# Thirteen units' second-order terms by seven block products, with softmax parts on GpSimd: an attention and MLP kernel on one core

## The chip, the cores and the metric

The program runs on one core of one Trainium2 chip. The metric is device time of one execution in microseconds (us). A core has TensorE (PE; PEld is its weight load), VectorE (DVE), ScalarE (ACT), GpSimd (POOL) and SyncE (SP, which here only starts transfers).

## The reference

Eight batches, eight heads, 576 tokens, 64 numbers per head; the inputs q and k are scaled by 200.

```
a = exp(phi - max(phi, axis=2)); a = a / (sum(a, axis=2) + 1e-09)        # 32 memory slots per head
k_m = einsum('bhsm,bhsd->bhmd', a, k); v_m = einsum('bhsm,bhsd->bhmd', a, v)
attn = softmax(q @ k_m.T / sqrt(64))                                      # over the 32 slots
x = (attn @ v_m), as 4608 tokens x 512
h = x @ w_in (512 x 2048);  g = h - tanh(h);  out = g @ w_out (2048 x 512)
```

## The kernel before

**Numbers in two halves.** Every float32 operand of the large products is kept as a float16 high part and a float16 low part (the rest), and a product is three products: high x high, high x low and low x high; low x low is left out. S_W, S_G and the like are powers of two that keep the parts in float16's range. The weights come as float64 bit patterns, and are turned into float32 and split in the start.

**Tiles.** Tokens go in 18 units of 256 (u), the 2048 inner columns in four blocks of 512 (fb). One *slot* is one pair (u, fb):
- *First product*, `mm1` (line 434): the weights are folded into the attention first (`att_p`, line 403, makes P = v_m w_in for a batch and fb), so h is P times the softmax: four column chunks k, six matmuls each over 256 tokens, into the accumulator tile h. There are two of these (pool `ps_h`, two buffers).
- *g = h - tanh(h)* by a polynomial: ScalarE squares h into u (line 450), VectorE makes h3 from h and u (458), ScalarE squares u once more (459), VectorE multiplies (464), ScalarE writes the float16 high part (466), VectorE the low part (471).
- *Second product*, `mm2` (line 483), for the slot two before: for each of two halves of 128 tokens and four chunks k, three matmuls of 512 columns (g high by w_out high and low, g low by w_out high) into the accumulators o0 and o1, which collect over the four fb of a unit. After the fourth ScalarE scales them to SBUF (line 516) and SyncE stores them.

**Order.** Up to the middle of unit 4 the order of all engines is written out as a list of words (START) and kept by `in_order`. T, E, L, K turn weights into float16 parts, i and o load them; H, a, b, c, M are first product, polynomial and second product. In this start units 0 to 3 keep partial sums in DRAM, which GpSimd's queue stores. From slot 18 on (unit 4, fb 2) a loop runs over the slots, and each batch's attention is hung in at slots before the batch's first: FX, FA, Q, KV load phi (twice), q, keys and values; X and Y take a maximum over phi, subtract it and apply exp; V pools keys and values (line 147, 80 matmuls); N, U, UV normalise and turn; S makes scores (187); A and B are the softmax (205 to 222); BH and BL its high and low parts (393, 399); P and PL make P (411 to 423). There the scheduler may order the instructions. The loop also reads all weights a second time (chk) and tests on ScalarE (309, 310) that none is out of the split's range; `squares_in`, `norms_in` and their like test norms. If a test fails, a wide path, not run here, does all in float32.

## Time and profile before

| | us |
|---|---|
| median of three runs | 696.89 |
| lowest, highest | 694.16, 697.13 |
| the profiled execution | 696.4 |
| its span, first to last instruction | 694.6 |
| TensorE busy | 664.5 |
| VectorE busy | 477.4 |
| ScalarE busy | 398.3 |
| GpSimd busy | 10.8 |

The span is divided into busy time per engine, into 40 slices, and into the chain of work that ended last. A group's row names line, engine, operation, output and inputs with their sizes, and behind the bar busy time, mean ns of one and the idle time in front. Matmuls overlap in the records: one of 512 columns is shown as 379 ns although the next starts 0.216 us after it, so the distance of starts is what counts.

### The profile page before, as it was taken

Reading aid. Unit: us, or ns where it says so; the run is one execution under the profiler, and the core shown is the slowest. Engines: PE = TensorE matmul, PEld = TensorE weight load, DVE = VectorE, ACT = ScalarE, POOL = GpSimd, SP = SyncE. Lnnn points to the kernel's source line nnn. Section 1 sums busy time; section 2 is a strip of 40 time slices with the busy share of each in tenths; the row PEclk is TensorE's granted clock in tenths of the full one; section 3 lists DMA queues with packets and bytes.
Section 4 is the critical chain, followed back from the end, with each engine's and each line's share of the span. In section 5 each row is a group of like instructions: output and inputs, shape, how many; then the busy total and the mean of one; then the engine's idle time right before and its main releaser. Section 6 shows DMA issues by size and latency. Waiting matters only on the chain.

```text
span 694.6 us, 13671 instructions
## 1 busy us (share of the span) xinstructions
PE 664.5 (96%) x5992; PEld 392.1 (56%) x5992; DVE 477.4 (69%) x571; ACT 398.3 (57%) x526; POOL 10.8 (2%) x26
## 2 busy tenths in 40 slices
PE   2688999999999999999999999999999999999996
PEld 2345574664656556666555655665566555666552
DVE  6699999998976596446596559556955695444541
ACT  3447666664545865665865595556645664544341
POOL 0000000001000000000000000000000000000000
PEclk9799999999999999999999999999999999999999
DMA  9955534682413940002940195009200300000001
GB/s 322 361 200 202 194 130 156 205 278 77 148 62 108 341 130 6 27 16 89 344 131 2 59 361 157 2 32 331 96 1 31 123 32 1 32 1 32 1 30 36
DMA packets 34003, 84.87 MB, mean 122 GB/s; under 512 B 3472, under 2 KB 8208, under 8 KB 33936
## 3 DMA queue, kind: packets, MB, share of 16 engines
q1 hardware_dynamic: 32512, 79.59, 33.3%
q0 software_dynamic: 1280, 4.20, 1.6%
q8 instruction: 49, 0.80, 0.5%
q14 instruction: 18, 0.15, 0.1%
q10 hardware_dynamic: 144, 0.13, 0.1%
HBM read 72.37 MB, written 11.53 MB: 121 GB/s over the span
## 4 chain that ended last, share of the span: by engine, by line
PE 78%; DVE 17%; DMA 3%; issue 1%; ACT 1%; SPq 0%; DVEq 0%
PE o L498 47%; PE h L444 22%; PE pkv L147 3%; PE pp L411 3%; DVE wt L264 2%; DVE wt L268 2%; DVE h L458 2%; DVE h L464 2%; DVE wt L260 1%; DMA kv<-in_kva_dram 1%; PE psc L187 1%; DVE g L471 1%; DVE ph L423 1%; DVE wout_lo L295 1%; DMA chk<-in_w_out_dram 1%
## 5 line engine op out<-in xcount | busy, mean ns | idle before, releaser
L498 PE MATMUL o<-wout_hi,g 128*128 128x512 f16 x1152 | 354.4, 379 | 0.8 <-ACT g L466 0.8
L498 PEld LDWEIGHTS <-g 128*128 128x128 f16 x1728 | 164.2, 98 | 206.9 <-issue 16.7
L498 PE MATMUL o<-wout_lo,g 128*128 128x512 f16 x576 | 218.4, 379 | 0.0
L444 PE MATMUL h<-ah,ph 128*128 128x256 f16 (+3 forms) x1536 | 201.2, 246 | 0.4 <-DVE h L458 0.4
L444 PEld LDWEIGHTS <-ph 128*128 128x128 f16 x2304 | 178.6, 98 | 28.9 <-issue 2.5
L444 PE MATMUL h<-al,ph 128*128 128x256 f16 (+3 forms) x768 | 170.1, 246 | 0.0
L458 DVE SCALAR_TENSOR_TENSOR h<-h,u 128x1024 f32<-128x1024 f32 x72 | 87.5, 1218 | 67.6 <-ACT u L450 67.6
L450 ACT ACTIVATE u<-h 128x1024 f32<-128x1024 f32 x72 | 73.2, 1018 | 91.5 <-PE h L444 91.5
L471 DVE TENSOR_TENSOR g<-h,g 128x1024 f16<-128x1024 f32 x70 | 85.3, 1221 | 49.8 <-ACT g L466 49.8
L466 ACT ACTIVATE g<-h 128x1024 f16<-128x1024 f32 x72 | 76.0, 1056 | 72.9 <-DVE h L464 72.9
L459 ACT ACTIVATE u<-u,beta 128x1024 f32<-128x1024 f32 x72 | 82.6, 1147 | 51.3 <-DVE h L458 50.6
L464 DVE SCALAR_TENSOR_TENSOR h<-u,h 128x1024 f32<-128x1024 f32 x72 | 87.9, 1221 | 25.8 <-ACT u L459 24.5
L423 DVE SCALAR_TENSOR_TENSOR ph<-pp,ph 128x1024 f16<-128x1024 f32 x32 | 38.9, 1216 | 2.4 <-ACT ph L418 2.4
L418 ACT ACTIVATE ph<-pp 128x1024 f16<-128x1024 f32 x32 | 32.5, 1016 | 1.9 <-PE pp L411 1.9
L516 ACT ACTIVATE ot<-o 128x512 f32<-128x512 f32 x35 | 20.5, 588 | 14.3 <-PE o L498 14.2
L147 PE MATMUL pkv<-kv,e 128*32 128x129 f32 (+1 forms) x640 | 25.6, 294 | 2.6 <-DMA kv<-in_kva_dram 2.2
L196 DVE STREAM_TRANSPOSE sc<-psc 128x288 f32<-128x288 f32 x32 | 13.5, 459 | 19.6 <-PE psc L187 19.6
L309 ACT ACTIVATE fy<-chk 128x512 f32<-128x512 f32 x32 | 21.4, 667 | 5.2 <-DMA chk<-in_w_in_dram 2.8
L310 ACT ACTIVATE fy<-fy,one 128x512 f32<-128x512 f32 x32 | 23.0, 719 | 0.7
L147 PEld LDWEIGHTS pkv<-kv,e 128*32 128x32 f32 (+1 forms) x640 | 17.1, 114 | 10.8 <-issue 5.9
L264 DVE SCALAR_TENSOR_TENSOR wt<-raw,wt 128x512 uint32<-128x512 uint32 x32 | 20.7, 688 | 0.0
L268 DVE SCALAR_TENSOR_TENSOR wt<-raw,wt 128x512 uint32<-128x512 uint32 x32 | 20.6, 687 | 0.0
(96 smaller groups left out, 372.3 us busy)
## 6 DMA issues: line engine op xcount, KB each, us to landing
kv<-in_kva_dram SPq DMA_DIRECT2D x32, 516.0 KB, 7.7
q<-in_qt_dram SPq DMA_DIRECT2D x16, 576.0 KB, 7.0
raw<-in_w_in_dram SPq DMA_DIRECT2D x16, 512.0 KB, 6.6
raw<-in_w_out_dram SPq DMA_DIRECT2D x16, 512.0 KB, 5.1
chk<-in_w_in_dram SPq DMA_DIRECT2D x16, 512.0 KB, 5.0
chk<-in_w_out_dram SPq DMA_DIRECT2D x16, 512.0 KB, 5.3
out_dram<-ot SPq DMA_DIRECT2D x27, 256.0 KB, 2.0
pt<-in_phx_dram SPq DMA_DIRECT2D x8, 576.0 KB, 4.4
```

The lines of the kernel that those rows point to most:

```text
L147: nc.tensor.matmul(pa[32 * h : 32 * h + 32, r, 0:129], e[0:K, c, 32 * hh : 32 * hh + 32], d["kv"][h][0:K, r, c, :], start=(c == 0), stop=( ...
L264: nc.vector.scalar_tensor_tensor(t, r[:, :, 0], 29, t, op0=ALU.logical_shift_right, op1=ALU.bitwise_or)
L268: nc.vector.scalar_tensor_tensor(t, r[:, :, 1], 0xC0000000, t, op0=ALU.bitwise_and, op1=ALU.bitwise_or)
L423: nc.vector.scalar_tensor_tensor(pl, pa, S_P / (S_V * S_W), ph, op0=ALU.mult, op1=ALU.subtract)
L444: nc.tensor.matmul(hp[:, k, tu : tu + w], px[:, g, cs], d[ax][:, g, ta : ta + w], start=(n == 0), stop=(n == 5),)
L450: nc.scalar.activation(uu, hp, AF.Square, scale=1.0 / (S_A * S_P))
L458: nc.vector.scalar_tensor_tensor(h3, hp, C2 * S_G / (S_A * S_P), uu, op0=ALU.mult, op1=ALU.mult)
L459: nc.scalar.activation(uu, uu, AF.Square, bias=c["beta"])
L464: nc.vector.scalar_tensor_tensor(h3, uu, CC, h3, op0=ALU.add, op1=ALU.mult)
L466: nc.scalar.activation(gg[:, 0], h3, AF.Copy)
L471: nc.vector.tensor_tensor(gg[:, 1], h3, gg[:, 0], op=ALU.subtract)
L498: nc.tensor.matmul(o, gx[:, k, P * tt : P * tt + P], wx[:, 4 * fb + k, :], start=(first and k == 0 and wx is wout_hi and gx is gh), stop=( ...
```

## The change

**Second product.** From unit 5 on `mm2_blocks` takes the place of `mm2`. High x high stays: 2 x 4 matmuls of 512 columns. The two second-order terms together are the product of a 2 x 2 block matrix by another: g in blocks by token half (th) and pair of chunks (kh), w_out by pair of chunks and column half (nh), both with a high and a low layer. Eight block products become seven, in Strassen's scheme, each of four matmuls of 256 columns: high of one side by low of the other and the reverse, for two chunks. Sums of w_out's blocks (`b_form`, words G in the start) are made once, on GpSimd, in float16, in tiles bt that take the place of the key and value buffers; sums of g's blocks (`a_forms`) in each slot, by four VectorE instructions on 512 float16 numbers per partition. Four of the products go into a tile x, which takes one of the two buffers of `ps_h`; first products keep one, hs. At a unit's end (`evict`) x is added to both accumulators' results: two copies on ScalarE, six steps on VectorE.

**GpSimd.** It makes g's low part, the softmax subtraction and division, the softmax's low part, phi's subtraction for batches 4 to 7, and the squares of the weight test.

**Plan.** The whole program keeps the written order. Attention of a batch is spread over 14 slots by a table, in halves: keys and values are loaded for the first half r = 0, pooled, and then for r = 1 into the same buffers; words before ";" stand behind the first product, those between ";" and "|" behind the second product's matmuls, the rest at the slot's end. Batch 3's phi maximum and first loads stand at the end of START. S_W and S_G are smaller powers of two.

```diff
-S_W = 2.0 ** 14
+S_W = 2.0 ** 13
-S_G = 2.0 ** 25
+S_G = 2.0 ** 23
...
-M31 L15 PL03 b02 T13 o13:gg H22 V2 N2 b12 H03 L13 c02 P13 c12 PL13 M02 a03 o12:pp4 U2 a22 T14 b03 H13 L14 c03
+PL03 b02 T13 o13:gg H22 V2 N2 b12 H03 L13 G00 c02 P13 c12 PL13 G01 M02 a03 o12:pp4 U2 G02 a22 T14 b03 H13 G03
...
+    def load_kv_half(self, b, d, r):
...
+        for g in range(2):
+            t = self.big.tile([P, 2, 5, 129], F32, tag="q", name=f"kv{b}{g}{r}")
+            for i in range(2):
+                nc.sync.dma_start(t[:, i, 0:4, :], ins["kva"][b, 2 * g + i, :, r])
+                nc.sync.dma_start(t[0:64, i, 4, :], ins["kvt"][b, 2 * g + i, :, r])
...
+    def expo_pool(self, b, d):
...
+        nc.scalar.activation(m[:, 0], d["px"][:, 0, 0:256], AF.Copy)
+        nc.gpsimd.tensor_tensor(e[:, 0:4, :], e[:, 0:4, :], m.to_broadcast((P, 4, 256)), op=ALU.subtract)
...
+    def soft_max(self, b, d, t):
...
+        nc.vector.tensor_reduce(m, s3, axis=AX.X, op=ALU.max)
+        nc.gpsimd.tensor_tensor(s3, s3, m.unsqueeze(2).to_broadcast((P, NB, 32)), op=ALU.subtract)
...
     def window(k):
...
-        nc.scalar.activation(y, hf, AF.Square)
+        nc.gpsimd.tensor_tensor(y, hf, hf, op=ALU.mult)
...
+    def g3_pool(u, fb):
+        h3, gg = gs[u, fb]
+        nc.gpsimd.tensor_tensor(gg[:, 1], h3, gg[:, 0], op=ALU.subtract)
...
+    def a_block(gg, th, kh):
+
+        return gg[:, :, 2 * kh : 2 * kh + 2, P * th : P * th + P]
+    def a_forms(u, fb):
+
+        gg = gs[u, fb][1]
+        a11, a21, a12, a22 = (a_block(gg, th, kh) for kh in range(2) for th in range(2))
+        f = big.tile([P, 2, 4, 2, P], F16, tag="uu", name=f"f{u}{fb}")
+        s4, s3, s1, s2 = (f[:, :, i] for i in range(4))
+        for o, x, y, op in ((s3, a21, a11, ALU.subtract), (s1, a21, a22, ALU.add), (s2, s3, a22, ALU.add), (s4, a12, s2, ALU.subtract)):
+            nc.vector.tensor_tensor(o, x, y, op=op)
...
+    def b_form(fb, i):
+
+        if i == 0:
+            bts[fb] = big.tile([P, 4, 2, 2, 256], F16, tag=f"kv{fb}", name=f"bt{fb}", bufs=1)
+        for n, w in enumerate((wout_hi, wout_lo)):
...
+            nc.gpsimd.tensor_tensor(t[:, i, n], x, y, op=ALU.subtract)
...
+    def mm2_blocks(u, fb, first, last):
...
+        def main(th):
+            for k in range(4):
+                nc.tensor.matmul(
+                    o[th], gg[:, 0, k, P * th : P * th + P], wout_hi[:, 4 * fb + k, :], start=(first and k == 0), stop=False
+                )
+
+        def prod(dst, a, b, new=False, end=False):
+            for kk in range(2):
+                for n in range(2):
+                    nc.tensor.matmul(
+                        dst, a(1 - n, kk), b(n, kk), start=(new and kk == 0 and n == 0), stop=(end and kk == 1 and n == 1)
+                    )
...
+        m1 = (x[:, 0, lo], ab(0, 0), bb(0, 0), first)
+        m2 = (o[0][:, lo], ab(0, 1), bb(1, 0))
+        m3 = (o[0][:, hi], af(0), bb(1, 1))
+        m4 = (o[1][:, lo], ab(1, 1), bf(3))
+        m5 = (x[:, 0, hi], af(2), bf(0))
+        m6 = (x[:, 1, lo], af(3), bf(1), first)
+        m7 = (x[:, 1, hi], af(1), bf(2))
+        if not last:
+            main(0)
+            main(1)
+            for m in (m2, m4, m1, m5, m6, m7, m3):
+                prod(*m)
+            return
...
+        for m, end in ((m1, False), (m5, True), (m6, False), (m7, True)):
+            prod(*m, end=end)
+        nc.scalar.activation(ra[:, 1], x[:, 0, lo], AF.Copy, scale=sc)
+        nc.scalar.activation(rb[:, 2], x[:, 0, hi], AF.Copy, scale=sc)
+        for th, ms in ((0, (m2, m3)), (1, (m4,))):
+            main(th)
+            for m in ms:
+                prod(*m, end=m is ms[-1])
...
+    def evict():
...
+        nc.vector.scalar_tensor_tensor(ra[:, 0], x[:, 1, lo], sc, ra[:, 1], op0=ALU.mult, op1=ALU.add)
+        nc.vector.scalar_tensor_tensor(rb[:, 0], x[:, 1, hi], sc, ra[:, 0], op0=ALU.mult, op1=ALU.add)
+        nc.vector.tensor_tensor(ra[:, 2], ra[:, 0], rb[:, 2], op=ALU.add)
+        nc.vector.tensor_tensor(rb[:, 1], rb[:, 0], rb[:, 2], op=ALU.add)
...
+            nc.vector.scalar_tensor_tensor(r, o[th], sc, r, op0=ALU.mult, op1=ALU.add)
+            nc.sync.dma_start(out[t0 + P * th : t0 + P * th + P, :], r)
...
+        (-11, "FQ{0} FA{0}"), (-10, "; X{0} KR{0}0"), (-9, "| XP{0} YM{0}"), (-8, "; YE{0} | V{0}0 KR{0}1 N{0}0"), (-7, "| V{0}1 N{0}1 QT{0}0"),
...
+        mm1(u, fb)
+        g1(u, fb)
+        do(0)
+        g1_square(u, fb)
+        if forms:
+            a_forms(*forms.pop())
+        g2(u, fb)
+        queue.append((u, fb))
+        v, vb = queue.pop(0)
+        (mm2 if v < 5 else mm2_blocks)(v, vb, vb == (2 if v in parts else 0), vb == NFB - 1)
+        while squared:
+            window_sum(*squared.pop(0))
+        do(1)
+        g2_high(u, fb)
+        g3_pool(u, fb)
+        while due:
+            step(due.pop(0), True)
+        evict()
+        if u > 4:
+            forms.append((u, fb))
+        do(2)
```

How it moves instructions, at three places. First TensorE in the second product of unit 16, fb 0 (g160 is that slot's g, high and low part; o1600 and o1601 are the accumulators). Before, 24 such pairs of a weight load and a matmul of 512 columns:

```order
L498 LDWEIGHTS g160_7111
L498 MATMUL o1600_7275<-wout_hi_96,g160_7111 128x512
...
L498 MATMUL o1600_7275<-wout_lo_97,g160_7111 128x512
...
L498 MATMUL o1601_7276<-wout_hi_96,g160_7111 128x512
...
L498 MATMUL o1601_7276<-wout_lo_97,g160_7111 128x512
```

Now eight pairs of the leading term and 28 of the products (bt0 holds sums of w_out's blocks, f160 sums of g's):

```order
L668 LDWEIGHTS g160_8065
L668 MATMUL o1600_8207<-wout_hi_96,g160_8065 128x512
...
L668 MATMUL o1601_8208<-wout_hi_96,g160_8065 128x512
...
L675 MATMUL o1600_8207<-wout_lo_97,g160_8065 128x256
...
L675 MATMUL o1601_8208<-bt0_1644,g160_8065 128x256
...
L675 MATMUL x_2678<-wout_hi_96,g160_8065 128x256
...
L675 LDWEIGHTS f160_8105
L675 MATMUL x_2678<-bt0_1644,f160_8105 128x256
...
L675 MATMUL o1600_8207<-wout_hi_96,f160_8105 128x256
```

The leading term stands ahead of all that needs g's low part, and the products that need the sums of the slot's g come last.

Second VectorE in the slot of unit 16, fb 1, in which unit 15 ends. Before, with the weight test's last steps between:

```order
L458 SCALAR_TENSOR_TENSOR h3161_7185<-h161_7158,u161_7183 128x1024
L346 TENSOR_REDUCE stat_65<-wn_6931 128x4
...
L464 SCALAR_TENSOR_TENSOR h3161_7185<-u161_7183,h3161_7185 128x1024
L471 TENSOR_TENSOR g161_7189<-h3161_7185,g161_7189 128x1024
L458 SCALAR_TENSOR_TENSOR h3162_7268<-h162_7241,u162_7266 128x1024
```

Now:

```order
L547 SCALAR_TENSOR_TENSOR h3161_8102<-hs_2679,u161_8100 128x1024
L583 TENSOR_TENSOR f160_8105<-g160_8065 128x2x256 x2
L583 TENSOR_TENSOR f160_8105<-f160_8105,g160_8065 128x2x256
L583 TENSOR_TENSOR f160_8105<-g160_8065,f160_8105 128x2x256
L556 SCALAR_TENSOR_TENSOR h3161_8102<-u161_8100,h3161_8102 128x1024
L724 SCALAR_TENSOR_TENSOR r150_8111<-x_2678,r150_8111 128x256
L725 SCALAR_TENSOR_TENSOR r151_8112<-x_2678,r150_8111 128x256
L726 TENSOR_TENSOR r150_8111<-r150_8111,r151_8112 128x256
L727 TENSOR_TENSOR r151_8112<-r151_8112 128x256
L735 SCALAR_TENSOR_TENSOR r150_8111<-o1500_7815,r150_8111 128x512
L735 SCALAR_TENSOR_TENSOR r151_8112<-o1501_7816,r151_8112 128x512
```

The low part has left the engine; the sums of the slot before stand between h3's two steps, and the unit's end behind them, ahead of the next slot's first step.

Third GpSimd in the start, behind the stores of partial sums (d). Before, stores alone:

```order
L522 DMA d30_1479<-ot310_1477 128x512
L522 DMA d31_1495<-ot311_1493 128x512
L522 DMA out_0_dram<-pr00_1676 128x512
L522 DMA out_0_dram<-pr01_1677 128x512
L522 DMA out_0_dram<-pr10_1866 128x512
```

Now (bt0 and bt1 are the sums of w_out's blocks for fb 0 and 1):

```order
L649 DMA d31_1495<-ot311_1493 128x512
L598 TENSOR_TENSOR bt0_1644<-wout_hi_96 128x512
L598 TENSOR_TENSOR bt0_1644<-wout_lo_97 128x512
L598 TENSOR_TENSOR bt0_1644<-wout_hi_96,bt0_1644 128x512
L598 TENSOR_TENSOR bt0_1644<-wout_lo_97,bt0_1644 128x512
...
L598 TENSOR_TENSOR bt1_1777<-wout_hi_96 128x512
L598 TENSOR_TENSOR bt1_1777<-wout_lo_97 128x512
L649 DMA out_0_dram<-pr00_1681 128x512
L649 DMA out_0_dram<-pr01_1682 128x512
```

Ten sums (four of the rows stand twice) come ahead of the first store of unit 0's result, and the rest among the later stores.

274 lines of the change are left out of this document (200 added, 74 removed), and 11 rows, old and new, of tables (PLAN, PLAN3, PLAN_C).

## The prediction

> **What bounds the kernel now.** I read the page first: busy time, the slices, and the chain that ended last.
>
> ```profile
> span 694.6 us, 13671 instructions
> PE 664.5 (96%) x5992; PEld 392.1 (56%) x5992; DVE 477.4 (69%) x571; ACT 398.3 (57%) x526; POOL 10.8 (2%) x26
> PE   2688999999999999999999999999999999999996
> DVE  6699999998976596446596559556955695444541
> PE 78%; DVE 17%; DMA 3%; issue 1%; ACT 1%; SPq 0%; DVEq 0%
> ```
>
> TensorE is busy in nine tenths of every slice from the fifth on, and 78% of the last chain is its own work. VectorE is full only until about 155 us. GpSimd does next to nothing. So there are two stages: a start in which VectorE is as full as TensorE, and from 155 us on a stage of TensorE alone. Whether anything else holds TensorE there is told by its waits between 215 and 690 us, of which the view knows one:
>
> ```profile
> PE psc L187 <- DVE sc L196: 0.3, 1, 0.3
> ```
>
> What one slot costs is read from the chain in order of time: one first product (24 matmuls of 256 columns), one second product (24 of 512), and the next second product's start, beside the pooling of two neighbouring batches.
>
> ```profile
> 393.89 2.75 PE pkv L147 x80
> 402.63 2.62 PE h L444 x24
> 465.56 2.75 PE pkv L147 x80
> 641.61 5.18 PE o L498 x24
> 649.41 5.18 PE o L498 x24
> ```
>
> A slot without attention is 649.41 - 641.61 = 7.80 us, exactly 2.62 + 5.18. A 256-column matmul with weights of its own costs 2.62 / 24 = 0.1092 us, one of 512 columns 5.18 / 24 = 0.2158 us: half the columns, 51% of the price. Eight slots with one batch's attention take 465.56 - 393.89 = 71.67 us, so 9.27 us of attention.
>
> **The change, part by part.** The sum is made against the profiled execution: 696.4 us, of which 694.6 are the span, 1.8 lie around it; the median of the runs is 696.89, 0.5 above it. A measurement of this kernel tells a change from none at about 0.5%, here 3.5 us.
>
> *The second product.* For the last 13 units of tokens, four second products each, 24 matmuls of 512 columns become 8 of 512 (the leading term) and seven products of four matmuls of 256 columns. By the two prices: 8 x 0.2158 + 28 x 0.1092 = 1.727 + 3.057 = 4.784 us, against 5.18: 0.396 less, times 13 x 4 = 52 is 20.6 us. Everything of this lies on the path, since TensorE waits for nothing there. The price holds for products as well: the first product also changes its accumulator every six matmuls and loads weights for each.
>
> *The forms and the hi/lo split.* Each slot's low half moves from VectorE to GpSimd, and four sums of float16 blocks come to VectorE. The chain from a first product to the low half, and what bounds the new steps, by the groups kept apart by shape (after the bar: busy us, mean ns of one, idle before):
>
> ```profile
> L464 DVE SCALAR_TENSOR_TENSOR h<-u,h 128x1024 f32<-128x1024 f32 x72 | 87.9, 1221 | 25.8 <-ACT u L459 24.5
> L458 DVE SCALAR_TENSOR_TENSOR h<-h,u 128x1024 f32<-128x1024 f32 x72 | 87.5, 1218 | 67.6 <-ACT u L450 67.6
> L471 DVE TENSOR_TENSOR g<-h,g 128x1024 f16<-128x1024 f32 x70 | 85.3, 1221 | 49.8 <-ACT g L466 49.8
> L459 ACT ACTIVATE u<-u,beta 128x1024 f32<-128x1024 f32 x72 | 82.6, 1147 | 51.3 <-DVE h L458 50.6
> L466 ACT ACTIVATE g<-h 128x1024 f16<-128x1024 f32 x72 | 76.0, 1056 | 72.9 <-DVE h L464 72.9
> L450 ACT ACTIVATE u<-h 128x1024 f32<-128x1024 f32 x72 | 73.2, 1018 | 91.5 <-PE h L444 91.5
> L295 DVE SCALAR_TENSOR_TENSOR wout_lo<-wt,wout_hi 128x512 f16<-128x512 f32 x16 | 10.3, 684 | 0.2
> masks.py:199 POOL TENSOR_SCALAR_AFFINE_SELECT ident<-ident 128x128 f32<-128x128 f32 x1 | 0.3, 283 | 0.0
> ```
>
> No elementwise step on GpSimd is in the trace. Bounds for one of 1024 elements: 1.22 us (VectorE's L471) and, from the only row of GpSimd with arithmetic, 8 x 0.283 = 2.26 us, doubled for two inputs 4.53. I take 2.26, the row of that engine. A float16 sum of 512 elements on VectorE: 0.34 (half of L295) to 0.68 us; I take 0.5. Then, from the end of a first product: 1.02 + 1.22 + 1.15 + 2.0 (sums of the slot before) + 1.22 + 1.06 + 2.26 = 9.9 us to the low half. Its own sums stand behind the next slot's h3, which ends at 7.40 + 1.02 + 1.22 = 9.6 us, so they end at about 11.9; the product that wants them starts two slots on, at 14.8. 2.9 us of cover: cost 0. Without the cover every microsecond over it costs 52.
>
> The first product now has one accumulator instead of two: it must be read by 1.02 + 1.22 = 2.24 us after its end and is written again 4.78 us after it. Cost 0, cover 2.5 us.
>
> *The unit's end.* Where a unit ends, ScalarE's two evictions become six steps on VectorE; the next unit's second product waits for the last two of them. Four run while the leading term is still being multiplied; the last two (0.68 us each, L295's size) end some 2.5 to 3.5 us after the product, and the next first product covers 2.62. Bounds 0 and 0.9 x 13 = 12 us; the second accumulator is wanted only 0.86 us after the first, so I take 0.5 us in all.
>
> *Attention.* Softmax subtraction and division, the low part and the phi subtraction go to GpSimd, in halves over 14 slots. VectorE loses work that nobody waited for: 0. But the pooling is cut in two, and its second half of keys and values is loaded into the buffers that the first half must leave. SyncE issues eight loads for it; how long eight issues take, and how long a load takes to land, is in its timeline and in the tile's view:
>
> ```profile
> 25.95 0.56 SPq L105 DMA_DIRECT2D kv<-in_kva_dram  x1
> 31.20 0.61 SPq L106 DMA_DIRECT2D kv<-in_kvt_dram  x1
> DMA to landing us min/median/max: 2.3/7.5/11.0
> ```
>
> Issues: 31.20 + 0.61 - 25.95 = 5.86 us; with the shortest landing 8.2 us after the first half, while the second starts 2.62 + 4.78 = 7.40 us after it. That is 0.8 us of waiting, with the median landing 6.0, and 0 if the last piece, wanted last, comes in time. Five batches: 0 to 30 us; I take 2, since the loads are half as large and alone in the queue. Five more changes of work on TensorE, 0.2 us each: 1.
>
> *The start.* 32 sums of weight blocks are put on GpSimd among the partial stores, from about 141 us on (the pooling of batch 2 frees their buffers). How full VectorE is there:
>
> ```profile
> 140.00:160.00 20.00, 19.24 (x172) 11.81 (x169) 19.77 (x27) 13.23 (x17) 0.00 (x0) 1.00 0.73 228
> 160.00:180.00 20.00, 20.00 (x163) 10.77 (x162) 16.41 (x24) 9.18 (x10) 2.16 (x4) 1.00 0.36 114
> 180.00:200.00 20.00, 20.00 (x206) 11.63 (x204) 17.39 (x22) 10.01 (x14) 1.08 (x2) 1.00 0.37 134
> 200.00:220.00 20.00, 20.00 (x239) 12.48 (x241) 14.05 (x14) 9.79 (x10) 1.08 (x2) 1.00 0.08 28
> ```
>
> VectorE (third pair) idles 0.23 + 3.59 + 2.61 + 5.95 = 12.4 us in 80. If GpSimd beside it slows it not at all, the start costs 0. 32 sums of 512 elements at 4 x 0.283 = 1.13 us are 36.2 us of GpSimd; if VectorE stood still in each, it would lag by 36.2 - 12.4 = 23.8 us. No row tells which. I take 3: the first ten sums alone fall where VectorE has no idle time, and a quarter of their 11.3 us is charged.
>
> The Trainium skill's page "SBUF — State Buffer", section "Who interferes with whom", speaks against the change here: a VectorE instruction with two SBUF inputs and a GpSimd instruction that reads SBUF shut each other out for their whole length. By it the sum would be that of the first rival below; the trace has no GpSimd arithmetic beside VectorE, so it neither agrees nor disagrees.
>
> *Sum.* 696.4 - 20.6 + 0.5 + 2 + 1 + 3 = **682.3 us**.
>
> **The rivals.**
>
> *VectorE and GpSimd take turns in the start.* Of VectorE's work between 141 and 161 us the share of lines that read two SBUF tensors, in the order 464, 471, 264, 268, 295:
>
> ```profile
> 141.00:161.00 20.00, 3.65 (x3) 1.00 0.73 228
> 141.00:161.00 20.00, 4.80 (x4) 1.00 0.73 228
> 141.00:161.00 20.00, 1.29 (x2) 1.00 0.73 228
> 141.00:161.00 20.00, 1.29 (x2) 1.00 0.73 228
> 141.00:161.00 20.00, 2.57 (x4) 1.00 0.73 228
> ```
>
> 13.6 of 19.8 us, 69%. If each of the 36.2 us of sums holds up that share, 25.0 us, less 12.4 of idle time, 12.6 us are left: 696.4 - 20.6 + 12.6 + 3.5 = 691.9 us. For it: the full VectorE row at 140. Against: a lag counts only beyond TensorE's lead. 14%: 9 faster, 5 within 0.5%.
>
> *Slower: GpSimd and VectorE take turns in the steady stage too.* Eight slots give GpSimd 8 x 1024 low halves, 6 x 576 of softmax, 1280 of phi and some 5.6 x 512 of window squares: 15,800 elements, 15.4 units of 1024. VectorE has 8 x (1.22 + 2.0) = 26 us on two SBUF tensors. Together 15.4 x 2.26 + 26 = 61 us, under the new 8 x 7.40 + 9.27 = 68.5. It decides from (71.7 - 26) / 15.4 = 2.97 us per 1024 elements on: then eight slots take longer than now. At 3.4 us, half way to the upper bound, 78.4 us, 6.7 more than now, 6.5 times: 740 us. For it: GpSimd's price is unmeasured. Against: in a plain slot its step falls where VectorE is idle. 6%. With it goes the load of keys and values at its worst, 30 us: 696.4 - 20.6 + 30 + 4.5 = 710 us, 4%.
>
> *It doesn't pay: small matmuls cost more here.* The gain is gone if a 256-column matmul costs (5.18 - 1.727) / 28 = 0.123 us: 696 to 703 us with the other costs, within 0.5% if some of them fall away. For it: their weights change tile between products. Against: the first product's 0.1092 with weights of its own. 6%.
>
> **How the numbers follow.** The forecast, 676 to 689 us, has 70%. Faster by over 0.5%: 70 + 9 = 79%. Within: 5 + 6 = 11%. Slower: 6 + 4 = 10%. The range begins a little under the sum with no new wait, 675.8 us (batch 3's maximum leaves the full stretch of VectorE, which may give 1 us), and ends at the first rival: 674.5 to 692.
>
> **What would show it.** Right: second products of about 4.78 us and plain slots of 7.40; 128x256 groups of the products at the first product's spacing; no wait of TensorE over 0.5 us for sums or low halves; GpSimd's 1024-element steps under 2.9 us; slot 18 starting within 3 us of before. Wrong: TensorE waiting for VectorE sums, for the second K/V half, or for accumulators at a unit's end; VectorE instructions of two SBUF inputs lengthened where GpSimd runs; a start that ends 5 us or more late.

## The result, and the profile after

The changed kernel takes **714.17 us** (median of four runs, 713.94 to 714.51), the kernel before 696.81 in the same runs (694.16 to 697.13): ratio 1.0258, 95% interval 1.0233 to 1.0283. It is slower by 2.6%, where 682.3 us was forecast and 692 was the end of the range. The profiled execution took 714.1 us, 712.3 of them the span. Of its page, the span, three rows of the slices, and the shares of the last chain:

```profile
span 712.3 us, 15574 instructions
DVE  6699999999797636796669776967697767768663
POOL 0000000274433123534243535353535255555421
PEclk9799999998879999999999999999999999999999
PE 58%; DVE 30%; ACT 4%; DMA 3%; issue 3%; SPq 1%; POOL 0%; DVEq 0%; ACTq 0%; POOLq 0%
```

VectorE has gone from 17% of the chain that ended last to 30%. GpSimd works from slice 8 of 40 on and has itself 0% of the chain: it does harm only through others. Where the time went is told by two marks. The first second product in blocks (unit 5, fb 0; before, the same slot's `mm2`), by its first matmul, before and after:

```profile
247.22 0.39 PE L498 MATMUL o<-wout_hi,g 128*128 128x512 f16 x1
```

```profile
L668 PE MATMUL o<-wout_hi,g x416: 376/379/390, 275.5 to 704.8; 128*128 128x512 f16 x139
```

So **28.3 us are lost ahead of the first block product**. From there on the changed kernel gains, but less than forecast: from the first product of slot 22 to that of slot 71 it takes 416.4 us, before 426.4; 10.0 gained, where 49 x 0.396 less 3.5 makes 15.9.

*The start.* The stretches from 140 to 220 us (busy time of PE, PEld, DVE, ACT, POOL; then the granted clock):

```profile
140.00:160.00 20.00, 14.89 (x149) 9.65 (x146) 19.93 (x21) 8.84 (x12) 15.90 (x10) 1.00 0.21 80
160.00:180.00 20.00, 14.59 (x91) 5.74 (x92) 17.59 (x16) 7.90 (x9) 7.80 (x8) 0.85 0.16 52
180.00:200.00 20.00, 18.07 (x110) 9.64 (x108) 16.50 (x10) 1.59 (x2) 12.62 (x13) 0.89 0.32 113
200.00:220.00 20.00, 11.67 (x109) 7.50 (x110) 17.21 (x20) 10.62 (x15) 1.81 (x2) 0.74 0.00 1
```

TensorE was busy 79.2 of these 80 us before and is now busy 59.2, at a granted clock down to 0.74. (In `sums_write_only` below, where GpSimd's steps don't read, it is 1.00 in all four stretches. How much of the loss the lower clock adds no run tells apart.) VectorE looks about as full as before, but in 180 to 200 it does 10 instructions instead of 22. Its timeline shows why (start, duration):

```profile
142.87 3.20 DVE L371 SCALAR_TENSOR_TENSOR wout_lo<-wt,wout_hi 128x512 f16<-128x512 f32 x2
171.06 5.50 DVE L256 TENSOR_TENSOR sc<-sc,sm 128x576 f32<-128x576 f32 x1
188.67 14.23 DVE L556 SCALAR_TENSOR_TENSOR h<-u,h 128x1024 f32<-128x1024 f32 x1
```

From 270 us on L556 takes 1.22 us each time. GpSimd's timeline beside the last of them, the first and the last of its 12 sums in a row:

```profile
188.48 1.16 POOL L598 TENSOR_TENSOR bt<-wout_hi 128x512 f16<-128x512 f16 x1
...
200.67 1.14 POOL L598 TENSOR_TENSOR bt<-wout_lo,bt 128x512 f16<-128x512 f16 x1
```

The sums come every 1.11 us from 188.48 to 201.81, as if nothing were beside them; VectorE's step begins 0.2 us after the first and ends 1.1 us after the last. ScalarE and TensorE wait behind it, as the waits from 140 to 240 us say (total, times, longest):

```profile
ACT g L561 <- DVE h L556: 26.7, 9, 18.4
...
PE pp L500 <- DVE sc L246: 8.9, 1, 8.9
```

*The steady stage.* The forecast prices held: a plain slot went from 7.80 to 7.40 us, by the chain in order of time (start, duration: first product, leading term, the seven products):

```profile
658.85 2.62 PE hs L533 x24
661.47 1.73 PE o L668 x8
663.19 0.87 PE o L675 x8
664.07 1.75 PE x L675 x16
665.81 0.44 PE o L675 x4
```

GpSimd's step of 1024 elements costs 2.16 us, where 2.26 was taken:

```profile
L570 POOL TENSOR_TENSOR g<-h,g 128x1024 f16<-128x1024 f32 x54 | 116.8, 2162 | 167.9 <-issue 81.9
```

What is missing is lost where a unit ends. TensorE's wait for the eviction, and VectorE's timeline at the end of unit 5 (slot 25), with GpSimd's beside it:

```profile
PE o L668 <- DVE r L735: 6.3, 5, 2.7
```

```profile
307.69 0.87 DVE L726 TENSOR_TENSOR r<-r,r 128x256 f32<-128x256 f32 x1
308.48 2.34 DVE L727 TENSOR_TENSOR r<-r 128x256 f32<-128x256 f32 x1
310.74 1.28 DVE L735 SCALAR_TENSOR_TENSOR r<-o,r 128x512 f32<-128x512 f32 x2
```

```profile
307.12 1.16 POOL L278 TENSOR_TENSOR sc<-sc,sz 128x576 f32<-128x576 f32 x1 [3.86 <-DVE sz L277]
308.24 2.30 POOL L570 TENSOR_TENSOR g<-h,g 128x1024 f16<-128x1024 f32 x1
```

L726 and L727, which take 0.42 us alone and read two tensors in SBUF, wait for GpSimd's softmax division and low half; L735, for which TensorE waits, comes behind them. At the end of unit 7 it is the sums of g that are held up, by two squares of the weight test that follow the low half, and the eviction stands behind them (VectorE, then GpSimd):

```profile
373.00 2.42 DVE L583 TENSOR_TENSOR f<-g 128x512 f16<-128x512 f16 x2 [0.17 <-POOL g L570]
```

```profile
370.83 2.14 POOL L570 TENSOR_TENSOR g<-h,g 128x1024 f16<-128x1024 f32 x1
372.93 2.22 POOL L385 TENSOR_TENSOR fy<-chk 128x512 f32<-128x512 f32 x2
```

By the distance from one first product's first matmul to the next, the slots behind a unit's end are longer than in a run without the wait (`end_first` below; for slot 66 `less_pool`) by 2.8 us (slot 26) and 0.9 each (slots 34, 42, 50, 66): 6.4 us, which agrees with the 6.3 us of the wait above.

### The profile page after: what moved, and what is told of

It is laid out like the page before. It is cut to its first block, busy times and chain, and to the rows that moved or that the text cites. A ratio compares the mean times of both kernels' runs of the same rounds, so it can differ in the third digit from the quotient of the medians.

```text
span 712.3 us, 15574 instructions
## 1 busy us (share of the span) xinstructions
PE 652.8 (92%) x6616; PEld 455.7 (64%) x6616; DVE 545.7 (77%) x815; ACT 372.5 (52%) x503; POOL 249.9 (35%) x182
## 4 chain that ended last, share of the span: by engine, by line
PE 58%; DVE 30%; ACT 4%; DMA 3%; issue 3%; SPq 1%; POOL 0%; DVEq 0%; ACTq 0%; POOLq 0%
PE hs L533 16%; PE o L668 11%; PE x L675 10%; PE o L675 8%; DVE h L556 6%; PE o L625 6%; DVE h L547 4%; PE pkv L189 3%; DVE f L583 2%; DVE wt L340 2%; DVE ph L512 2%; DMA kv<-in_kva_dram 2%; DVE g L566 2%; DVE wt L344 2%; PE pp L500 2%
## 5 line engine op out<-in xcount | busy, mean ns | idle before, releaser
L570 POOL TENSOR_TENSOR g<-h,g 128x1024 f16<-128x1024 f32 x54 | 116.8, 2162 | 167.9 <-issue 81.9
L533 PE MATMUL hs<-ah,ph 128*128 128x256 f16 (+3 forms) x1088 | 145.8, 248 | 0.0
L547 DVE SCALAR_TENSOR_TENSOR h<-hs,u 128x1024 f32<-128x1024 f32 x52 | 63.6, 1222 | 104.0 <-ACT u L539 103.9
L533 PE MATMUL hs<-al,ph 128*128 128x256 f16 (+3 forms) x544 | 122.1, 248 | 0.0
L625 PE MATMUL o<-wout_hi,g 128*128 128x512 f16 x320 | 101.5, 389 | 8.7 <-ACT g L561 7.4
L668 PE MATMUL o<-wout_hi,g 128*128 128x512 f16 x416 | 100.6, 379 | 6.3 <-DVE r L735 6.3
L556 DVE SCALAR_TENSOR_TENSOR h<-u,h 128x1024 f32<-128x1024 f32 x72 | 101.0, 1402 | 6.9 <-ACT u L552 6.9
L675 PEld LDWEIGHTS <-f 128*128 128x128 f16 x832 | 81.4, 98 | 9.4
L675 PE MATMUL x<-bt,f 128*128 128x256 f16 x624 | 76.6, 273 | 0.0
L625 PE MATMUL o<-wout_lo,g 128*128 128x512 f16 x160 | 62.4, 390 | 1.3 <-DVE wout_lo L371 1.3
L583 DVE TENSOR_TENSOR f<-g 128x512 f16<-128x512 f16 x104 | 55.9, 578 | 3.9 <-POOL g L570 3.9
L533 PE MATMUL h<-ah,ph 128*128 128x256 f16 (+2 forms) x448 | 57.1, 246 | 0.9 <-DVE h L547 0.9
L649 POOL DMA_DIRECT2D d<-ot x8 | 5.5, 689 | 131.5 <-ACT ot L643 131.5
```

The costliest lines, as they stand in the source:

```text
L533: nc.tensor.matmul(hp[:, k, tu : tu + w], px[:, g, cs], d[ax][:, g, ta : ta + w], start=(n == 0), stop=(n == 5),)
L547: nc.vector.scalar_tensor_tensor(h3, hp, C2 * S_G / (S_A * S_P), uu, op0=ALU.mult, op1=ALU.mult)
L556: nc.vector.scalar_tensor_tensor(h3, uu, CC, h3, op0=ALU.add, op1=ALU.mult)
L570: nc.gpsimd.tensor_tensor(gg[:, 1], h3, gg[:, 0], op=ALU.subtract)
L583: nc.vector.tensor_tensor(o, x, y, op=op)
L625: nc.tensor.matmul(o, gx[:, k, P * tt : P * tt + P], wx[:, 4 * fb + k, :], start=(first and k == 0 and wx is wout_hi and gx is gh), stop=( ...
```

## The experiments

**Whose fault is the start?** Four kernels, each with one edit, the last of them in the kernel before.

`sums_on_vector`:
```diff
-            nc.gpsimd.tensor_tensor(t[:, i, n], x, y, op=ALU.subtract)
+            nc.vector.tensor_tensor(t[:, i, n], x, y, op=ALU.subtract)
```


> The 32 sums of w_out's blocks run on VectorE, at the same places of the order. Theory (a run of GpSimd sums shuts VectorE's instructions with two SBUF inputs out until the run is over, which costs 28 us of the start): the 28.3 us are gone; VectorE pays 32 x 0.42 = 13.4 us itself, of which 12.4 us were idle time: 714.2 - 28.3 + 1 to 8 = 687 to 694 us, and no VectorE instruction of the start over 3 us. Rival (the order of the start, with batch 3's first steps in it, or the sums' tiles cause the lag, whatever engine sums): 708 us or more.

Measured: 696.07 us, ratio to before 1.0012 (0.9995 to 1.0029); the first block product starts at 257.0 us, 18.5 earlier. 2 us above the theory's range: against the next kernel's 244.7, VectorE pays 12.3 of its own 13.4 us, so its idle time hid next to nothing.

`sums_write_only`:
```diff
-            nc.gpsimd.tensor_tensor(t[:, i, n], x, y, op=ALU.subtract)
+            nc.gpsimd.memset(t[:, i, n], 0.0)
```


> In place of each sum GpSimd writes zeros into the same tile (so the four products that use sums of w_out are wrong); same count of instructions, same waits, no SBUF read. Theory: reading is what shuts VectorE out, so the lag goes: 714.2 - 28.3 = 686 us, VectorE's L556 at 1.22 us throughout the start. Rival A (any GpSimd instruction on SBUF does it): still over 700 us. Rival B (order or waits of the start): 714 us.

Measured: 683.91 us in a single run; the first block product starts at 244.7 us. The lag is gone with the reads, while GpSimd's 32 instructions and their waits are all there. Rivals A and B fall.

`sums_spaced`:
```diff
+        gap = big.tile([P, 512], F16, tag="gap", name=f"gap{fb}{i}", bufs=1)
...
             nc.gpsimd.tensor_tensor(t[:, i, n], x, y, op=ALU.subtract)
+            nc.gpsimd.memset(gap, 0.0)
+            nc.gpsimd.memset(gap, 0.0)
```


> Behind each sum GpSimd writes zeros twice into a spare tile (512 float16 numbers), which keeps it from starting the next sum at once; results unchanged. Theory of the whole run: VectorE gets in between two sums, no VectorE instruction waits over about 2 us, the lag falls below the 12.6 us of taking turns: 686 to 699 us. Rival (turns one by one, each sum holding up one instruction, as forecast in the first rival): every sum still costs what it did: 710 to 716 us.

Measured: 700.21 us in a single run, first block product at 260.8: 14.7 of the 28.3 us come back from doing more on GpSimd. Against `sums_write_only` 16.1 us are left. The time is 1 us above the theory's range, since turns cost more than its 12.6; but the sums now come about 2.2 us apart instead of 1.11, so they lie beside VectorE for twice as long. The longest wait of L556 is now one sum:

```profile
188.93 2.18 DVE L556 SCALAR_TENSOR_TENSOR h<-u,h 128x1024 f32<-128x1024 f32 x1
```

`before_plus_sums`:
```diff
-PL03 b02 T13 o13:gg H22 V2 N2 b12 H03 L13 c02 P13 c12 PL13 M02 a03 o12:pp4 U2 a22 T14 b03 H13
+PL03 b02 T13 o13:gg H22 V2 N2 b12 H03 L13 G00 c02 P13 c12 PL13 G01 M02 a03 o12:pp4 U2 G02 a22 T14 b03 H13 G03
...
+        "G": b_form,
```


> The kernel before, with the 32 sums on GpSimd at the changed kernel's places of the start and nothing else; their results are not used. Theory: the start loses about 28 us by these alone: 696.8 + 28 = 725 us, slot 18 some 28 us later. Turns one by one: 696.8 + 12.6 = 709 us. Rival (the rest of the change delays the start): 697 us.

Measured: 721.06 us in a single run, against a median of 695.09 for the kernel before, taken with it: 26 us from the sums alone. The same step waits as long (here it has line 465):

```profile
185.61 14.25 DVE L465 SCALAR_TENSOR_TENSOR h<-u,h 128x1024 f32<-128x1024 f32 x1
```

So GpSimd's reads are shown to be the cause of the start's loss, and a run of them costs more than turns.

**What makes a whole run shut VectorE out?** Five kernels that do none of the reference's work. Each test starts N GpSimd sums of 512 float16 numbers at a known moment and gives VectorE steps beside them, mostly with two SBUF inputs.

`bursts`:
```diff
+    for n in (0, 1, 2, 4, 8, 16):
+        test(0, two, add, n)
+    test(2, two, add, 8)
+    for f in (psum, one, small):
+        test(0, f, add, 8)
+    test(0, two, fill, 8)
```


> None of the reference's work: zeros are written to the output, and ahead of it eleven little tests run, each of N GpSimd sums of 512 float16 numbers beside six VectorE steps. With N = 0, 1, 2, 4, 8, 16 beside steps of 1024 float32 with two SBUF inputs; N = 8 started behind two such steps; N = 8 beside steps that read PSUM and SBUF, one SBUF tensor, and two float16 SBUF tensors of 512; and eight GpSimd writes of zeros. Theory (a burst holds VectorE's two-SBUF instruction until it is over): the first step takes 1.22 + N x 1.13 us, 10 us at N = 8, the others 1.22; the PSUM and the one-tensor steps and those beside writes take their own time. Rival (turns): steps and sums alternate, each of the six at most 1.13 us longer, whatever N. Where VectorE's steps are queued ahead of the burst (N = 8 behind two), the first long burst of the changed kernel's start alternated, so turns are expected there by both.

Measured, six steps beside 0, 4 and 16 sums (the sixfold row's time is that of all six):

```profile
7.53 7.51 DVE L49 SCALAR_TENSOR_TENSOR h<-u,h 128x1024 f32<-128x1024 f32 x6
33.31 10.83 DVE L49 SCALAR_TENSOR_TENSOR h<-u,h 128x1024 f32<-128x1024 f32 x6
59.90 11.66 DVE L49 SCALAR_TENSOR_TENSOR h<-u,h 128x1024 f32<-128x1024 f32 x6
```

Strict turns: every step in competition 0.83 us longer (11.66 - 7.51 = 4.15 for five of them), however many sums stand behind. Steps that read PSUM (7.51) and steps beside eight writes of zeros (7.52) lose nothing. Not only steps with two SBUF inputs are slowed, though. In the changed kernel a TENSOR_SCALAR with a single SBUF input takes longer too, here a pair ahead of the start's first burst and a pair in it:

```profile
137.69 0.75 DVE L336 TENSOR_SCALAR wt<-raw 128x512 uint32<-128x512 uint32 x2
153.57 2.61 DVE L336 TENSOR_SCALAR wt<-raw 128x512 uint32<-128x512 uint32 x2
```

Beside GpSimd's writes in `sums_write_only` the same pair takes 0.76 us. The theory of the whole run fell in `bursts`; the next four kernels looked for what the kernel's bursts had that the test's had not.

`bursts_first`:
```diff
+    late = [psum, two, two_more, two_more]
+    for n in (2, 4, 8, 16):
+        test(late, [add] * n)
```


> None of the reference's work, zeros to the output. As bursts, but GpSimd comes first: VectorE first does one step that reads PSUM (1.22 us), beside which the burst begins, and then its steps. With 2, 4, 8, 16 sums beside three steps of 1024 float32 with two SBUF inputs; 16 sums beside four pairs of a PSUM step and a two-input step; 8 sums beside three one-input steps, and beside three float16 sums of 512; 8 sums with two writes of zeros behind each; and four steps of 1024 float32 between two sums. Theory (whoever finds the other at work waits, and a run of GpSimd instructions without a gap never lets go): the first two-input step ends with the burst: about 1.2, 3.4, 7.9 and 17 us longer at 2, 4, 8 and 16, the later ones 1.22; with zeros between, at most 2.4 us. Rival (turns also here, as in bursts): the first step at most 1.2 us longer, at 16 sums as at 2; then the 14.23 us of the kernel's start have another cause.

Measured: turns again; the first step takes 1.27 us at every count, the two behind it 2.07 each at 4 sums or more.

`bursts_phase`:
```diff
+    for first_ in ((256,), (512,), (768,), (1024,), (1024, 256), (1024, 512), (1024, 768), (1024, 1024)):
+        test([lambda n=n: psum(n) for n in first_] + [two, two_more, two_more], [add] * 8)
```


> None of the reference's work, zeros to the output. Eight GpSimd sums beside three VectorE steps with two SBUF inputs (1024 float32), eight times; ahead of the steps VectorE reads PSUM for a time that grows from test to test (256, 512, 768, 1024, 1024 + 256, 1024 + 512, 1024 + 768, 2 x 1024 numbers: about 0.4 to 2.4 us), so that the first two-input step asks at another point of a running sum each time; in bursts_first it asked 0.05 us before a sum's end, in the kernel's start in the middle of one. Theory (a step that asks while a sum is running freely stays out until the burst ends): in the tests that ask mid-sum the first step takes 6 to 9 us; where it asks at a sum's end, 1.3 us. Rival (turns at any point): at most 2.4 us in all eight; then the kernel's sums differ from the test's in something else, for example in their operands, which lie in rows 256 numbers apart.

Measured: 1.24 to 2.07 us for the first step, at every moment of asking. The moment does not matter.

`bursts_free`:
```diff
+    def add(i):
+        nc.gpsimd.tensor_tensor(ts[i], a, b, op=ALU.subtract)
...
+        (1, 8, (512,)), (2, 8, (512,)), (3, 4, (512,)), (3, 8, (512,)), (3, 12, (512,)),
```


> None of the reference's work, zeros to the output. In the three tests before, all sums wrote one tile: they started 1.23 us apart and took 1.15, so 0.08 us lay between two. The changed kernel's sums write different pieces and started 1.11 us apart at 1.15 us each, so each began before the last was over. Here the sums go round one, two or three output tiles (1 x 8 sums, 2 x 8, 3 x 4, 3 x 8, 3 x 12), VectorE's two-input steps asking in the middle of a sum; then 3 tiles x 8 with the step asking at other points, and with the step asking first. Theory (overlap shuts VectorE out): with one tile turns, 2.1 us a step; with three tiles the first step takes about 5, 9 and 13 us at 4, 8 and 12 sums, and the two behind it 1.22. Rival (turns here too): at most 2.4 us a step at any count; then what sets the kernel's bursts apart stays open.

Measured: the overlap doesn't matter either; with three tiles the first step takes 1.86 us at 4, 8 and 12 sums.

`bursts_store`:
```diff
+    def store():
+        nc.vector.scalar_tensor_tensor(pr, pm[:, 0:DM], 1.0, pr, op0=ALU.mult, op1=ALU.add)
...
+        nc.gpsimd.dma_start(out[P * r : P * r + P, :], pr)
...
+    test(False, sums(rows, 8))
+    test(True, sums(lambda i: add(i % 3), 8))
+    test(True, sums(rows, 8))
+    test(True, sums(rows, 12))
+    test(True, sums(rows, 4))
+    test(False, sums(rows, 8), busy=True)
+    test(True, sums(rows, 8), busy=True)
+    test(True, [f for i in range(8) for f in (lambda i=i: rows(1 + i % 2), fill, fill)])
+    test(False, sums(rows, 8))
```


> None of the reference's work, zeros to the output. Nine tests of GpSimd sums of 512 float16 numbers beside three VectorE steps with two SBUF inputs. What is left that the kernel's bursts had and the tests so far had not: operands in two rows of 256, a store that GpSimd issues right ahead of the burst (the 5.50 and the 14.23 us followed one; the first burst, which took turns, did not), and TensorE and ScalarE at work. The tests: rows x 8; store and contiguous x 8; store and rows x 8, x 12, x 4; rows x 8 with TensorE and ScalarE busy; the same with a store; store and rows x 8 with two writes of zeros behind each; rows x 8 once more. Theory 1 (the store makes it): the first step takes 8 to 10 us in the tests with a store and 8 sums, 13 at 12, 4 to 5 at 4, under 3 with writes between, 2 in the others. Theory 2 (the rows make it): also without a store. Theory 3 (the other engines make it): only in the two busy tests. Rival: 2.1 us everywhere; then it stays open what sets the kernel's bursts apart.

Measured, the first step of the tests two to eight, in order:

```profile
28.37 9.94 DVE L54 SCALAR_TENSOR_TENSOR h<-u,h 128x1024 f32<-128x1024 f32 x1
44.26 9.81 DVE L54 SCALAR_TENSOR_TENSOR h<-u,h 128x1024 f32<-128x1024 f32 x1
60.09 14.23 DVE L54 SCALAR_TENSOR_TENSOR h<-u,h 128x1024 f32<-128x1024 f32 x1
80.40 5.38 DVE L54 SCALAR_TENSOR_TENSOR h<-u,h 128x1024 f32<-128x1024 f32 x1
90.60 1.58 DVE L54 SCALAR_TENSOR_TENSOR h<-u,h 128x1024 f32<-128x1024 f32 x1
105.27 9.84 DVE L54 SCALAR_TENSOR_TENSOR h<-u,h 128x1024 f32<-128x1024 f32 x1
121.14 2.08 DVE L54 SCALAR_TENSOR_TENSOR h<-u,h 128x1024 f32<-128x1024 f32 x1
```

**The store makes it.** Where GpSimd has issued a store right ahead of the sums, VectorE's step waits for all of them: 5.38, 9.81 and 14.23 us at 4, 8 and 12, the last to the hundredth what the changed kernel shows. Without one (90.60, and the first and the last test) it takes turns, with other engines busy or not, rows or not; with writes between the sums it takes turns behind a store too (121.14). The moment of asking is not the difference: in the tests with a store the step asks up to 0.17 us after the first sum's start, and `bursts_phase`, whose first test asks 0.16 us after it without a store, had turns (2.07 us). In the changed kernel the bursts at 169.24 and 188.48 us follow stores of L649 at once, and the first burst, which took turns, follows a wait for TensorE's pooling. Why a store does it, by its issue or by the transfer, no run tells; stores on another queue weren't tried.

**The steady stage.** Lengths of some slots, us, from one first product's first matmul to the next:

| slot | changed | end_first | less_pool | squares_only | evict_psum | best2 |
|---|---|---|---|---|---|---|
| 26 (behind unit 5's end) | 11.13 | 8.34 | 12.06 | 11.07 | 8.68 | 8.34 |
| 34 (behind unit 7's end) | 9.18 | 8.28 | 8.29 | 8.28 | 9.17 | 8.28 |
| 36 | 9.75 | 10.85 | 9.76 | 9.76 | 9.76 | 9.76 |
| 38 | 8.97 | 10.54 | 8.97 | 8.97 | 8.97 | 8.97 |
| 58 | 8.38 | 8.27 | 9.67 | 9.57 | 8.36 | 8.37 |

`end_first`:
```diff
+        ends = v > 4 and vb == NFB - 1
+        if forms and not ends:
+            a_forms(*forms.pop())
+        g2(u, fb)
...
+        evict()
+        if forms and ends:
+            a_forms(*forms.pop())
...
             step(due.pop(0), True)
-        evict()
```


> The changed kernel with one thing moved: in the slot in which a unit ends, VectorE does the six eviction steps right behind L556, ahead of the softmax steps and of the sums of g's blocks, so that they run before GpSimd's next burst. Start unchanged (mm2_blocks from 275.5 us on). Theory (11 unit ends lose some 9 of the forecast 20.6 us, since the eviction steps come late on VectorE, behind sums of g that GpSimd shuts out or in GpSimd's burst itself): TensorE's waits for r at L735 go, 5 to 9 us less, 705 to 709 us. Rival (the small matmuls' own price, or the K/V loads, took the rest): 712 to 715 us.

Measured: 722.26 us, ratio 1.0385 (1.0365 to 1.0405), 8 us slower than the changed kernel. The waits for r are nearly gone, and others have come (waits of TensorE from 240 to 706 us):

```profile
PE pp L500 <- DVE kvn L214: 4.0, 3, 1.5
...
PE o L668 <- DVE r L735: 1.3, 1, 1.3
```

VectorE had no slack to give: in the changed kernel it works without a pause from 373 to 394 us, slots 34 to 36. At slot 33 the profiled run of `end_first` is 3.2 us ahead of the changed kernel's. With the eviction first, TensorE comes 3.9 us earlier to slot 36 (389.1 for 393.0), but VectorE's softmax maximum in it only 2.4 (391.05 for 393.41), and with it, on GpSimd, the low half and the phi subtraction (395.08 for 397.45); TensorE now waits for exp of phi and for the normalised keys. Moving the eviction moved the wait to the attention, and made it longer. This expectation was wrong.

`less_pool`, and `squares_only` with the last pair of lines alone:
```diff
-        nc.gpsimd.tensor_tensor(s3, s3, m.unsqueeze(2).to_broadcast((P, NB, 32)), op=ALU.subtract)
+        nc.vector.tensor_tensor(s3, s3, m.unsqueeze(2).to_broadcast((P, NB, 32)), op=ALU.subtract)
...
-        nc.gpsimd.tensor_tensor(s3, s3, z.unsqueeze(2).to_broadcast((P, NB, 32)), op=ALU.mult)
+        nc.vector.tensor_tensor(s3, s3, z.unsqueeze(2).to_broadcast((P, NB, 32)), op=ALU.mult)
...
-        nc.gpsimd.tensor_tensor(y, hf, hf, op=ALU.mult)
+        nc.scalar.activation(y, hf, AF.Square)
```


> The changed kernel with softmax subtraction and division back on VectorE and the weight test's squares back on ScalarE; the low half, phi's subtraction and the softmax's low part stay on GpSimd, and the order of the program is the same. Theory A (at unit ends GpSimd's bursts of two or three steps hold up the sums and the eviction): the bursts are down to one step, 4 to 7 us less, 707 to 710 us. Theory B (the order alone, six steps behind all else, costs it): VectorE has 0.76 us more per softmax step ahead of the eviction, so 713 to 717 us.

> The changed kernel with the weight test's squares back on ScalarE and nothing else. Theory (at the unit ends of slots 33, 41, 49 and 65 the squares follow the low half on GpSimd without a gap and hold up the sums of g, and behind them the eviction): slots 34, 42, 50 and 66 lose their 0.9 us each, as in less_pool; slot 58 gains 1 us, since the norms' copy stands behind the squares on ScalarE: 711 to 712 us. Rival (it was the softmax steps that less_pool moved): 714 us, slots 34 to 66 as in the changed kernel.

Measured: 711.38 us, ratio 1.0219 (1.0183 to 1.0255), and 711.9, ratio 1.0254 (1.0226 to 1.0282): both near the changed kernel's ratio, so the slots decide. Both give slot 34 (and 42, 50, 66) back and lose 1.2 to 1.3 us in slot 58: the squares do it, the softmax steps nothing of it. The 4 to 7 us of theory A didn't come: with the softmax steps back on VectorE slot 26 takes 12.06 us, 1 us more than with the squares alone. The two sums of g that took 2.42 us take 0.76 in `squares_only`:

```profile
372.81 0.76 DVE L583 TENSOR_TENSOR f<-g 128x512 f16<-128x512 f16 x2
```

`evict_psum`:
```diff
-        nc.vector.tensor_tensor(ra[:, 2], ra[:, 0], rb[:, 2], op=ALU.add)
-        nc.vector.tensor_tensor(rb[:, 1], rb[:, 0], rb[:, 2], op=ALU.add)
+        nc.vector.scalar_tensor_tensor(ra[:, 2], x[:, 0, hi], sc, ra[:, 0], op0=ALU.mult, op1=ALU.add)
+        nc.vector.scalar_tensor_tensor(rb[:, 1], x[:, 0, hi], sc, rb[:, 0], op0=ALU.mult, op1=ALU.add)
```


> The changed kernel with the two eviction steps that read two SBUF tensors (L726, L727) made to read the accumulator x in PSUM instead; one copy on ScalarE falls away. Same order. Theory A (the burst shuts out steps with two SBUF inputs only): L727's 2.34 us at the first unit's end becomes 0.42, TensorE's wait there shrinks from 2.7 to about 0.7 us, elsewhere nothing: 711 to 713 us. Rival B (the steps are late by their place in the order): 714 us; the trace tells them apart by the length of that step.

Measured: 709.87 us, ratio 1.0206 (1.0188 to 1.0223), a little better than theory A's range. With nothing moved, the step that took 2.34 us takes 0.41, and TensorE's step comes at 308.44 instead of 310.74 us:

```profile
308.10 0.41 DVE L726 SCALAR_TENSOR_TENSOR r<-x,r 128x256 f32<-128x256 f32 x1
308.44 1.27 DVE L734 SCALAR_TENSOR_TENSOR r<-o,r 128x512 f32<-128x512 f32 x2
```

**Versions.** Places for the 32 sums on VectorE, with and without the other edits.

`late_vector_end` is `end_first` with the sums in slots 18 to 24; `late_end_less_pool` is that with `less_pool`'s edits:
```diff
+    PLAN_G = ((18, "G00 G01"), (19, "G02 G03"), (20, "G10 G11"), (21, "G12 G13"), (22, "G20 G21"), (23, "G22 G23"), (24, "G30 G31 G32 G33"))
```


> The sums of w_out's blocks on VectorE, spread over slots 18 to 24 (four a slot, 1.7 us, where VectorE idles half of the time), and the unit's end as in end_first. Theory: the start is that of the kernel before (mm2_blocks from about 245 to 249 us on), and from there 429.3 us less 5 to 9: 676 to 684 us in all, faster than the kernel before by 11 to 19. Rival (the sums cost VectorE as much there as in the start, 12 us): 688 to 696 us.

> As late_vector_end, with softmax subtraction and division on VectorE and the squares on ScalarE too. Theory A (bursts of GpSimd still cost something once the unit's end is first): 1 to 4 us under late_vector_end. Theory B (the waits are gone already and VectorE's own 0.76 us per step is hidden): within 1 us of it. Theory C (VectorE's added steps come between h3 and its uses): 1 to 4 us above.

Measured: 705.32 us, ratio 1.0132 (1.0112 to 1.0153), and 699.93, ratio 1.0056 (1.0038 to 1.0073). Slot 18 starts at 204.3 us, so the start is whole; but the eviction edit keeps its cost, and slots 23 to 25 take 10.64, 10.92 and 14.06 us instead of 9.02, 8.36 and 7.46: the last sums meet batch 3's attention on VectorE. `late_vector_end` missed the ranges of theory and rival alike; `late_end_less_pool` is 5.4 us under it, more than the 4 of its theory A.

`sums_in_slots`:
```diff
+    for b in range(NFB):
+        tasks.setdefault(18 + b, []).append("| " + " ".join(f"G{b}{i}" for i in range(4)))
```


> The changed kernel with one thing moved: the 32 sums of w_out's blocks leave GpSimd and the start, and stand on VectorE at the ends of slots 18 to 21, eight a slot (8 x 0.42 = 3.4 us; VectorE was busy 7.0 us of the 20 from 240 to 260). All else is the change as it was. Theory (the start's 28.3 us come from the sums alone, and from their place; late_vector_end lost its 10 us in slots 23 to 26, where its last sums met batch 3's attention): slot 18 starts at about 204 us, slots 19 to 35 take what they took in the changed kernel: 714.2 - 29.8 = 684 us, 682 to 687. Rival (VectorE has no room for them in these slots either): 690 to 696 us.

Measured: 691.26 us, ratio 0.9921 (0.9894 to 0.9948). The start is whole (slot 18 at 206.3), but slots 24 and 26 take 13.18 and 12.81 us instead of 8.36 and 11.13. In slot 24 batch 3's softmax, which shares VectorE with the last sums, comes late (TensorE waits 2.1 us for its low part alone). Slot 26 is not the sums' doing: TensorE waits the same 2.7 us for the eviction as in the changed kernel, but here the granted clock behind the wait was 0.73 (288.7 to 295.1 us), there 1.00 (310.6 to 316.3), and the eight matmuls of the leading term took 3.07 us instead of 1.89. `sums_write_only`, with no sums on either engine, shows the same (12.48 us, clock 0.77). The start came out as the theory said, the time as the rival said.

`best`:
```diff
-        (0, "P{0}2 PL{0}2 ; AM{0}1 | AE{0}1"), (1, "; AD{0}1"), (2, "P{0}3 PL{0}3 ; AT{0}1"), (3, "AS{0}1"),
+        (0, "P{0}2 PL{0}2 ; AM{0}1 | AE{0}1"), (1, "| AD{0}1"), (2, "P{0}3 PL{0}3 ; AT{0}1"), (3, "AS{0}1"),
```


> sums_in_slots, less_pool and evict_psum together, and at the first unit's end batch 3's softmax division behind the eviction. Theory: 684.4 for the sums, 2.8 less by less_pool, 3 to 4 less in slot 26, where less_pool still waited: 676 to 680 us, faster than the kernel before by 2 to 3%. Rival (as with end_first, a wait removed makes another chain late): 681 to 688 us.

`best2`:
```diff
+    for sl, words in ((18, "| G00 G01 G02 G03 G10 G11"), (19, "| G12 G13 G20 G21 G22 G23"), (20, "; G30 G31 G32 G33")):
+        tasks.setdefault(sl, []).append(words)
...
+        if late:
+            nc.gpsimd.tensor_tensor(y, hf, hf, op=ALU.mult)
+        else:
+            nc.scalar.activation(y, hf, AF.Square)
...
-                squared.append(window(chk.pop(0)))
+                squared.append(window(chk.pop(0), sl >= 54))
```


> Of best: sums of w_out's blocks on VectorE in slots 18 (12), 19 (12) and 20 (8, ahead of batch 3's scores), squares on ScalarE up to slot 53 and on GpSimd from 54 on, eviction from PSUM, batch 3's division behind the eviction; softmax subtraction and division stay on GpSimd, as in the changed kernel. Theory (slots 23 and 24 lost 1.9 us in best since the last sums stood ahead of batch 3's softmax; slots 37, 45, 58, 60 lost 0.2 to 1.0 by softmax on VectorE and squares on ScalarE): 682.8 less 2 to 4, 679 to 681 us. Rival (a burst of low half and softmax division holds up a unit's end again): 682 to 686 us.

Measured: `best` 682.77 us, ratio 0.9810 (0.9796 to 0.9824); `best2` **681.17 us**, ratio 0.9807 (0.9785 to 0.9828). Both beat both kernels, and can't be told from each other. `best` came out in its rival's range, `best2` 0.2 us above its theory's. In `best2` the first block product starts at 246.4 us, before 247.2, and one wait for the eviction is left:

```profile
L670 PE MATMUL o<-wout_hi,g x416: 376/379/390, 246.4 to 670.5; 128*128 128x512 f16 x139
```

```profile
PE o L670 <- DVE r L736: 1.2, 1, 1.2
```

## Why the prediction was wrong

*Second product: right.* 0.40 us a slot against 0.396 forecast; the rival that small matmuls cost more is out. `best2`, where most of the two costs below is out of the way, takes 1.1 us less than the forecast: the idea pays about what the sum said. That the totals agree so closely is in part chance, since `best2` has other costs than the sum (the sums on VectorE, squares on ScalarE).

*The start: the step that failed.* "if VectorE stood still in each, it would lag by 36.2 - 12.4 = 23.8 us. No row tells which. I take 3". It cost 28.3, more than the upper bound. That bound took for granted that a sum in progress holds up VectorE for its own length at most, and that VectorE's idle time makes good a part of the lag. In the runs the sums' reads cost 30.8 us against `sums_write_only`. About half of that was turns (16.1 us are left in `sums_spaced`), and the rest, which came back there, steps that waited for a whole burst behind a store, other engines with them. The idle time paid for next to nothing: on VectorE itself the sums cost 12.3 of their 13.4 us (`sums_on_vector`). The 3 was a quarter of a price for which no row stood, taken from the harmless side; the profile's full VectorE row at 140 us spoke for the other end.

*The first rival* had the right engines and the wrong size: its turns make 12.6 us, and `sums_spaced`, where turns are all that is left, lost 16.3 us of its time against `sums_write_only` (a single run each, and with the sums spread over twice the time). The Trainium skill's page "SBUF — State Buffer", section "Who interferes with whom", by which the rival was weighed, has each shut out for one whole instruction. `bursts` agrees (a step 0.83 us longer per turn, none beside writes or from PSUM); behind a store the measurement goes further than the page: 14.23 us for 12 instructions. There the measurement decides.

*The unit's end: mis-sized.* 0.5 us was taken between bounds of 0 and 12; it cost 6.4. The six steps themselves are as long as forecast (0.42 and 0.68 us), but the prediction let them begin with the product. They begin behind the sums of g and the softmax steps of the same slot, and each of those with two SBUF inputs can wait for a GpSimd step of 1.2 to 2.3 us (`evict_psum`, `squares_only`).

*K/V halves and changes of work: right in sum, as a remainder.* 3 us forecast. The ten gained between slots 22 and 71 are 19.4 less 6.4 for the unit ends less 3.0, which is what is left; no run measured it by itself. The second half's load was waited for in slot 29 alone, about 0.9 us.

*GpSimd's price and the steady rival: right.* 2.16 us per 1024, under the 2.97 from which turns would have decided.

With the two sizes measured, the working gives 696.4 - 20.6 + 28.3 + 6.4 + 3 = 713.5 us, against 714.1; since the 3 is confirmed by a remainder alone, that is a balance and no test.

## What to carry to other kernels

Before work goes to an idle GpSimd, list what VectorE does beside it with two SBUF inputs (or in a TENSOR_SCALAR with one), and what GpSimd issues just ahead: a run of reading steps behind a GpSimd store held VectorE for the run's whole length. Let a step that others wait for read PSUM, or keep GpSimd's runs short and apart. And where a term has no row and its bounds are 20 us apart, the forecast is a choice between them, not a quarter of the way.
